# A new order for the opening of all five engines, three small inputs in one load, and the last product cut by columns

## The chip, the cores and the metric

The kernel runs on one core of one Trainium2 chip. A core has five engines that run side by side: TensorE (PE in the profile, with its weight loads as PEld), VectorE (DVE), ScalarE (ACT), GpSimd (POOL) and SyncE (SP), which here issues nearly all transfers. The metric is the time of one execution on the device, in microseconds (us); lower is better.

## The reference

Windowed attention over 8 batches, 8 heads, 576 positions and 64 dimensions, and then a dense block on its output (4608 tokens of 512, inner size 1024):

```python
scores = scale * np.matmul(q, k.transpose(0, 1, 3, 2))
mask_plain = (rel >= 0) & (rel < 32)                       # heads 0 to 3
mask_dil = (rel >= 0) & (rel < 128) & (rel % 4 == 0)       # heads 4 to 7
attn = softmax(np.where(mask, scores, -1e9)); x = attn @ v # to (4608, 512)

h = x @ w_in
sm = softmax(h); solu = h * sm
ln = (solu - mean) / sqrt(var + 1e-6) * g_ln
out = (ln @ w_out).astype(np.float32)
```

The two weights arrive as 64-bit floats. They have to be turned into 32-bit floats on the chip, by their bits.

## The kernel before

**Units.** The attention is 32 units (a batch and two heads each). The steps of unit n are written as words: `q` loads q and k, `v` loads v, `S` is the scores on PE (the mask first, as a product of the 16-bit identity `id_bf` with `mask_sb`, then 40 small products), `max`, `sub`, `exp`, `sum`, `inv`, `norm` the softmax, `turn` a transpose on VectorE (`pt`), `V` the product with v, `xh` and `xl` the split of its result into a high part on ScalarE (`x_hi`) and a low part (`x_lo`). Scores of units 0 to 4 all lie in banks 2 and 3 of the accumulator, later ones in banks 6 and 7; so `S` of a unit waits until the scores of the unit before are read. Three tuples say who does a step: units in `ACT_SCORES` have their scores copied by ScalarE (`cp`) and the maximum subtracted by GpSimd, all others have that subtraction (L291) on VectorE; units in `POOL_X` have `xl` on GpSimd after a copy by ScalarE (`xc`); blocks in `DVE_LOW` have `lo` on VectorE and all others on GpSimd.

**Weights.** They are 16 blocks, `w0` to `w7` of w_in and `w8` to `w15` of w_out, of 128 rows and 512 64-bit numbers, which is 1024 floats in a load. Each goes through `abs` and `low` (ScalarE), `clamp`, `sign` and `join` (VectorE), for w_out `gain` with the factors g (ScalarE), `hi` (ScalarE) and `lo`. The sign is taken out of the upper 16-bit quarter and written as 16-bit numbers:

```python
def conv_sign(b):
    upper = words[b].bitcast(U16).rearrange("p (n four) -> p n four", four=4)[:, :, 3]
    nc.vector.tensor_scalar(
        out=cv[b]["low"].bitcast(U16).rearrange("p (n two) -> p n two", two=2)[:, :, 1],
        in0=upper, scalar1=SIGN_BIT, scalar2=None, op0=ALU.bitwise_and,
    )
```

`SLOTS` gives each block the buffer that it is loaded to: a later block waits until its buffer's last one is converted.

**Token tiles.** The dense block is 36 tiles of 128 tokens: `ha` and `hb` are the first 512 columns of h (first and last half of the inner sum), `hc` and `hd` the others; h of tiles 0 and 2 lies in banks 0 and 1, of the other tiles up to 15 in banks 2 and 3. Then come `peak`, `e` and `gate` (which reads the banks for the last time), `mid`, `var`, `forth` and `back` (out to memory and back in another order), `trA`/`trB`, `thA`/`thB`, `tlA`/`tlB` (transpose, high and low part by halves), `o` (24 products of 512 columns with w_out) and `out`. From tile 16 on, pairs of tiles share products of half size (L733).

**Order.** Nothing is scheduled by the framework: each engine does its work in the order in which the words are written. `OPENING` is one long list of words for all five engines, up to unit 11 and tile 7; behind it the loops run `STEP` and `PAIR`, and `LAST_PAIR` for tiles 34 and 35. A list thus sets five queues at once, and a wait on an engine holds up all that stands behind it there. SyncE issues loads in the order of the list; at most eight are on their way.

## Time and profile before

| what | value |
|---|---|
| time, median of 3 runs | 502.91 us (501.33 to 503.94) |
| profiled execution: its time | 504.69 us |
| profiled execution: its span, first to last instruction | 502.8 us |
| granted clock of TensorE | 1.00 |
| busy: PE, DVE, ACT, POOL | 469.9, 351.4, 291.3, 298.7 us |
| transfers | 94.14 MB, 187 GB/s on average |

The profile is one execution. A row of a timeline has the start and the length in us, the engine, the line of the kernel, the operation, what it writes and reads, its shapes and how many; in brackets stands how long the engine was idle ahead of it, and what ended that. A row of a group has the same with the busy time and the mean of one in ns. "PE banks L255" are score products, "PE banks L333" the products with v, L247 the masks, L401 tiles of h, L531 the products with w_out. The chain of work is followed back from the last instruction, at each step to what released it; "issue" in it is time in which the engine waited for nothing that the profile shows.

### The profile page before, as it was taken

How to read it: one execution, taken by the hardware profiler on the slowest of the kernel's cores; microseconds unless marked ns; L12 is line 12 of the kernel's file. 1: busy time of each engine (PE TensorE's matmuls, PEld its weight loads, DVE VectorE, ACT ScalarE, POOL GpSimd, SP SyncE). 2: the span in 40 equal slices, each digit the busy share in tenths (PEclk: the TensorE clock that was granted, in tenths of full speed). 3: DMA queues.
4: the chain of work that ended last, by engine and by line, in shares of the span. 5: the costliest groups of instructions: out<-in, count | busy, mean ns of one | idle time of the engine just before them, and what ended most of it. 6: DMA issues, size and time to landing. Idle time of an engine off the chain costs nothing.

```text
span 502.8 us, 16542 instructions
## 1 busy us (share of the span) xinstructions
PE 469.9 (93%) x7064; PEld 376.0 (75%) x7064; DVE 351.4 (70%) x619; ACT 291.3 (58%) x483; POOL 298.7 (59%) x367
## 2 busy tenths in 40 slices
PE   1457998999999999999999999999999999999996
PEld 1336776788878888788878787878787888888875
DVE  3996989867627788777868686868676865445562
ACT  3766897744424444534457575757575767666551
POOL 1652776556533765778976666665756555766440
PEclk9999999999999999999999999999999999999999
DMA  7979175664465655666667677676765545354461
GB/s 280 402 254 359 37 261 163 230 190 133 137 193 156 194 164 169 186 175 178 201 175 216 206 211 211 210 211 211 212 210 164 160 129 146 104 168 124 113 188 63
DMA packets 51337, 94.14 MB, mean 187 GB/s; under 512 B 5952, under 2 KB 26048, under 8 KB 51264
## 3 DMA queue, kind: packets, MB, share of 16 engines
q1 hardware_dynamic: 50544, 92.43, 59.6%
q8 instruction: 55, 0.90, 0.8%
q10 hardware_dynamic: 720, 0.66, 0.4%
q14 instruction: 18, 0.15, 0.1%
HBM read 60.04 MB, written 28.31 MB: 176 GB/s over the span
## 4 chain that ended last, share of the span: by engine, by line
PE 91%; DMA 5%; issue 2%; DVE 1%; ACT 0%; SPq 0%; DVEq 0%; ACTq 0%
PE banks L531 40%; PE banks L733 20%; PE banks L401 18%; PE banks L333 7%; PE banks L255 6%; DMA qt<-qT 2%; DMA raw<-w_in 2%; DMA kt<-kT 1%; DVE pt L317 0%; PE banks L247 0%; DVE x_lo L388 0%; DVE nmax L412 0%; SPq L232 0%; DVE rs L302 0%; ACT sm L285 0%
## 5 line engine op out<-in xcount | busy, mean ns | idle before, releaser
L531 PE MATMUL banks<-w_o,th 128*128 128x512 f32 x576 | 179.9, 393 | 0.0
L522 POOL TENSOR_TENSOR tl<-t,th 128x512 fp32r<-128x512 f32 x68 | 87.9, 1305 | 59.9 <-ACT th L516 59.8
L531 PEld LDWEIGHTS banks<-w_o,th 128*128 128x128 f32 x576 | 106.6, 188 | 22.6 <-ACT th L516 0.6
L531 PE MATMUL banks<-w_o,tl 128*128 128x512 f32 x288 | 112.5, 391 | 0.0
L401 PE MATMUL banks<-w_i,x_hi 128*128 128x512 f32 x256 | 82.8, 405 | 0.2 <-DVE mu L436 0.2
L531 PEld LDWEIGHTS banks<-w_o,tl 128*128 128x128 f32 x288 | 54.0, 188 | 12.3 <-DVE tl L522 0.9
L516 ACT CAST th<-t 128x512 fp32r<-128x512 f32 x72 | 43.4, 621 | 23.5 <-DVE t L508 16.1
L401 PEld LDWEIGHTS banks<-w_i,x_hi 128*128 128x128 f32 x256 | 47.2, 191 | 11.1 <-DVE mu L436 0.8
L508 DVE STREAM_TRANSPOSE t<-raw 128x512 f32<-128x512 f32 x72 | 46.9, 684 | 6.1 <-DMA out<-ob 3.0
L401 PE MATMUL banks<-w_i,x_lo 128*128 128x512 f32 x128 | 50.7, 396 | 0.0
L333 PEld LDWEIGHTS banks<-pt,vt 32*64 32x64 f32 x2816 | 35.3, 138 | 20.0 <-issue 12.8
L452 ACT ACTIVATE e<-t 128x1024 f32<-128x1024 f32 x35 | 37.0, 1058 | 17.6 <-DVE t L448 17.3
L294 POOL TENSOR_TENSOR sm<-sm,mx 128x640 f32<-128x640 f32 x27 | 34.5, 1276 | 21.4 <-DVE mx L281 18.8
L333 PE MATMUL banks<-pt,vt 32*64 32x64 f32 (+3 forms) x2816 | 38.8, 234 | 8.6 <-issue 5.4
L298 ACT ACTIVATE sm<-sm 128x640 f32<-128x640 f32 x32 | 23.6, 739 | 35.8 <-POOL sm L294 35.1
L255 PEld LDWEIGHTS banks<-kt,qt 64*32 64x32 f32 x2560 | 29.8, 112 | 17.7 <-issue 10.7
L269 DVE TENSOR_TENSOR sm<-banks,mask_sb 128x640 f32<-128x640 f32 x22 | 18.1, 824 | 35.1 <-PE banks L255 35.0
L255 PE MATMUL banks<-kt,qt 64*32 64x64 f32 x2560 | 35.7, 238 | 5.6 <-issue 4.1
L544 ACT ACTIVATE ob<-banks,rstd 128x512 f32<-128x512 f32 x35 | 24.0, 686 | 24.8 <-issue 16.6
L757 DVE CUSTOM_DVE_ANT_0 t<-banks,t 128x512 f32<-128x512 f32 x30 | 20.7, 690 | 22.3 <-PE banks L733 16.9
L751 ACT COPY t<-banks 128x512 f32<-128x512 f32 x30 | 17.6, 588 | 30.3 <-PE banks L733 30.3
L427 ACT ACTIVATE e<-t,nmax 128x1024 f32<-128x1024 f32 x19 | 21.9, 1153 | 18.8 <-DVE nmax L764 18.2
(151 smaller groups left out, 868.5 us busy)
## 6 DMA issues: line engine op xcount, KB each, us to landing
mid<-t SPq DMA_DIRECT2D x140, 128.0 KB, 2.4
raw<-mid SPq DMA_DIRECT2D x34, 512.0 KB, 3.9
vt<-vw SPq DMA_DIRECT2D x32, 384.0 KB, 3.9
kt<-kT SPq DMA_DIRECT2D x32, 312.0 KB, 4.4
qt<-qT SPq DMA_DIRECT2D x32, 296.0 KB, 4.7
out<-ob SPq DMA_DIRECT2D x35, 256.0 KB, 2.7
x_hi<-x SPq DMA_DIRECT2D x12, 288.0 KB, 3.5
t<-w_in SPq DMA_DIRECT2D x5, 512.0 KB, 7.8
```

Source lines behind the costliest of these rows:

```text
L255: nc.tensor.matmul(out=ps[WIN * c : WIN * c + WIN, h, WQ * i : WQ * i + WQ], lhsT=qt[D * h : D * h + D, q0 : q0 + WIN], rhs=kt[D * h : D * ...
L294: eng.tensor_tensor(out=st[n]["sm"], in0=st[n]["sm"], in1=wide(mx), op=ALU.subtract)
L298: nc.scalar.activation(out=sm, in_=sm, func=AF.Exp, scale=0.125)
L333: nc.tensor.matmul(out=ps_x[D * h : D * h + D, c, c0 : c0 + k1 - k0], lhsT=vt[WIN * c : WIN * c + WIN, i, D * h : D * h + D], rhs=pt[WIN * ...
L401: nc.tensor.matmul(out=ps_h(i)[:, half], lhsT=a[:, kt, xs], rhs=w_i[:, kt, half, part, :], start=(kt == 0 and k == 0), stop=(kt == KT - 1 ...
L452: nc.scalar.activation(out=e, in_=t, func=AF.Square, accum_out=per_tile(i, "sq"))
L508: nc.vector.transpose(out=turned(i)[:, cut(c)].rearrange("p k (a r) -> p k a r", r=WIN), in_=ms[i]["mv"].rearrange("p (a k s) -> p k a s", ...
L516: nc.scalar.copy(out=ms[i]["th"][:, cut(c)], in_=turned(i)[:, cut(c)])
L522: eng.tensor_tensor(out=ms[i]["tl"][:, cut(c)], in0=turned(i)[:, cut(c)], in1=ms[i]["th"][:, cut(c)].bitcast(F32), op=ALU.subtract,)
L531: nc.tensor.matmul(out=ps_o(i), lhsT=a[:, f, :], rhs=w_o[:, f, part, :], start=(f == 0 and k == 0), stop=(f == FT - 1 and k == 2), skip_gr ...
L544: nc.scalar.activation(out=ob, in_=ps_o(i), func=AF.Copy, scale=rstd)
L733: nc.tensor.matmul(out=banks[:, bank], lhsT=left(pa, kt), rhs=right(pb, kt), start=j in (1, 2, 5) and kt == 0 and k == 0, stop=kt == 1 and ...
```

## The change

The kernel's arithmetic stays, but for the order of the last sums. Four things change: the list `OPENING` is another one, for all five engines; the tuples beside it have other members; the 16-bit identity, both masks and g come in one load `pack`, and the 32-bit identity, which nothing reads, is gone; and the last `o` (tile 35) is done by halves of columns, the left half into bank 0 and the right half into bank 1. The left half goes out while the right half is multiplied; the right half goes out in two quarters, by ScalarE and VectorE, each with its own tile and its own queue (ACT and SP).

```diff
-ACT_SCORES = (1, 5, 7, 8, 9)
-POOL_X = (0, 4, 5)
-DVE_LOW = (12, 13, 14, 15)
+ACT_SCORES = (2, 5, 6)
+POOL_X = (4, 5)
+DVE_LOW = (13,)
...
-    "w1 ib abs1 w3 m0 low1 q0 clamp1 w0 sign1 w2 abs3 q1 low3 q2 join1 hi1 S0 sign3 clamp3 "
...
+    "pack q0 S0 w0 q1 max0 sub0 low0 abs0 w3 exp0 abs3 S1 q2 clamp0 low3 sign0 sum0 w2 inv0 "
...
-    "oA.b oB.b out.b "
+    "oL.b outL.b oR.b outR.b "
...
+    packed = const.tile([P, P // 2 + NS * WQ + FT], F32, name="packed")
+    id_bf = packed[:, 0 : P // 2].bitcast(BF16)
+    mask_sb = packed[:, P // 2 : P // 2 + NS * WQ].bitcast(BF16).rearrange("p (d c) -> p d c", d=2)
+    g_sb = packed[:, P // 2 + NS * WQ :]
...
+    def moe_o_half(i, half):
+        th, tl = ms[i]["th"], ms[i]["tl"]
+        cols = slice(DO // 2 * half, DO // 2 * half + DO // 2)
+        for f in range(FT):
+            for k, (a, part) in enumerate(((th, 0), (th, 1), (tl, 0))):
+                nc.tensor.matmul(
+                    out=banks[:, half, cols],
+                    lhsT=a[:, f, :],
+                    rhs=w_o[:, f, part, cols],
...
+    def moe_out_part(i, half, cols, on_act):
+        if half == 0:
+            ob = moe.tile([P, DO], F32, name="ob", bufs=1)
+        else:
+            ob = att.tile([P, 2, NS, WQ], F32, name=f"sm{int(on_act)}")
...
+        if on_act:
+            nc.scalar.activation(out=ob[:, cols], in_=ps[:, cols], func=AF.Copy, scale=rstd)
+            nc.scalar.dma_start(out=rows[:, cols], in_=ob[:, cols])
         else:
...
+            nc.sync.dma_start(out=rows[:, cols], in_=ob[:, cols])
...
+    def out_right(i):
+        moe_out_part(i, 1, slice(DO // 2, DO * 3 // 4), True)
+        moe_out_part(i, 1, slice(DO * 3 // 4, DO), False)
```

Lines behind the edit have other numbers: the scores are L252 after (L255 before), the sign L828 (L803), the clamp L821 (L796), the join L836 (L811), `sub` on VectorE L288 (L291), `max` L278 (L281), `turn` L314 (L317), the products with w_out L528 (L531) and, by halves, L549.

SyncE at the start of the program, before. `t`, `raw` and `tp` with w_in or w_out are blocks of the weights (t1 is w1, t3 w3, t0 w0, t2 w2), sizes are partitions x 32-bit floats (16-bit for the identity and the mask):

```order
L232 DMA t1_98<-w_in 128x1024
L833 DMA id_bf_83<-ident_bf 128x128
L232 DMA t3_103<-w_in 128x1024
L835 DMA mask_sb_81<-mask 128x320
L209 DMA kt0_109<-kT 128x624
L210 DMA qt0_108<-qT 128x592
L232 DMA t0_113<-w_in 128x1024
L232 DMA t2_116<-w_in 128x1024
L209 DMA kt1_121<-kT 128x624
L210 DMA qt1_120<-qT 128x592
```

The same place after:

```order
L857 DMA packed_80<-pack 128x392
L206 DMA kt0_97<-kT 128x624
L207 DMA qt0_96<-qT 128x592
L229 DMA t0_142<-w_in 128x1024
L206 DMA kt1_145<-kT 128x624
L207 DMA qt1_144<-qT 128x592
L229 DMA t3_156<-w_in 128x1024
L206 DMA kt2_204<-kT 128x624
L207 DMA qt2_203<-qT 128x592
L229 DMA t2_213<-w_in 128x1024
L229 DMA t1_222<-w_in 128x1024
L229 DMA raw4_227<-w_in 128x1024
```

The first k and q moved from the fifth and sixth place to the second and third; w1, once the first, is the eleventh now. Behind these stand w4 (the last row), v0, w7, q3, w10, w9, w5, v1, w6, v2, v3 and q4.

VectorE around the subtraction of unit 3 and the transpose of unit 2, before (`mx`, `sm`, `rs` belong to the softmax, `mag` and `low` to the weights, `pt0_590` is unit 2's transpose):

```order
L281 TENSOR_REDUCE mx_467<-banks_90 128x10
L302 TENSOR_REDUCE rs_475<-sm0_337 128x10
L291 TENSOR_TENSOR sm1_478<-banks_90,mx_467 128x640
L306 TENSOR_SCALAR rs_475<-rs_475 128x10
L307 RECIPROCAL rs_475<-rs_475 128x10
L811 SCALAR_TENSOR_TENSOR mag2_437<-mag2_437,low2_335 128x512
L302 TENSOR_REDUCE rs_540<-sm1_478 128x10
L306 TENSOR_SCALAR rs_540<-rs_540 128x10
L307 RECIPROCAL rs_540<-rs_540 128x10
L388 TENSOR_TENSOR x_lo_89<-banks_90,x_hi_88 128x576
L317 STREAM_TRANSPOSE pt0_590<-sm0_337 128x640
```

and after (`pt0_510` is unit 2's transpose):

```order
L385 TENSOR_TENSOR x_lo_86<-banks_87,x_hi_85 128x576
L278 TENSOR_REDUCE mx_433<-banks_87 128x10
L821 TENSOR_SCALAR mag1_424<-mag1_424 128x512
L828 TENSOR_SCALAR low1_426<-raw5_370 128x512
L836 SCALAR_TENSOR_TENSOR mag0_356<-mag0_356,low0_362 128x512
L836 SCALAR_TENSOR_TENSOR mag1_424<-mag1_424,low1_426 128x512
L828 TENSOR_SCALAR low3_367<-t0_245 128x512
L821 TENSOR_SCALAR mag3_437<-mag3_437 128x512
L288 TENSOR_TENSOR sm1_502<-banks_87,mx_433 128x640
L385 TENSOR_TENSOR x_lo_86<-banks_87,x_hi_85 128x576
L314 STREAM_TRANSPOSE pt0_510<-sm0_296 128x640
```

Six instructions on weights stand now between the maximum of unit 3 and its subtraction; before, one other stood there. Ahead of that subtraction VectorE has 38 instructions besides three fills in both programs, but others: after, the scores of units 0 to 2 come ahead of most of the weights.

PE at the scores of units 8 and 9, after (kt0 and qt0 are unit 8's, kt1 and qt1 unit 9's):

```order
L398 MATMUL banks_87<-w_i_83,x_lo_86 128x512
L244 LDWEIGHTS packed_80
L244 MATMUL banks_87<-packed_80 128x320
L252 MATMUL banks_87<-kt0_1170,qt0_1169 32x64 x40
L244 LDWEIGHTS packed_80
L244 MATMUL banks_87<-packed_80 128x320
L252 MATMUL banks_87<-kt1_1283,qt1_1282 32x64 x40
L398 MATMUL banks_87<-w_i_83,x_hi_85 128x512 x2
```

S9 follows S8 at once here, with `ha5` behind it. Before, hc4, V7, ha4, hd4 and hb4 stood between the two, and o0 behind S9. Up to V2 the order of PE is the same in both programs (S0, S1, S2, V0, S3, V1, S4, V2); behind it come ha1 hc0 V3 ha0 hb0 before, and ha0 hc1 hc0 V3 ha1 hb0 after. V6 and V7 stand together now, ahead of hc4.

More of the change, by code (lines that the diff above doesn't have):

```diff
@@ L138, in windowed_attention_then_solu_kernel @@
     w_out: bass.AP,
-    g_ln: bass.AP,
-    mask: bass.AP,
-    ident: bass.AP,
-    ident_bf: bass.AP,
+    pack: bass.AP,
     out: bass.AP,
@@ L542, in moe_out @@
         rows, rstd = out[i * P : i * P + P, :], ms[i]["rstd"]
-        if i < NTILE - 1:
-            nc.scalar.activation(out=ob, in_=ps_o(i), func=AF.Copy, scale=rstd)
-            nc.sync.dma_start(out=rows, in_=ob)
-        else:
-            left, right = slice(0, DO // 2), slice(DO // 2, DO)
-            nc.scalar.activation(
-                out=ob[:, left], in_=ps_o(i)[:, left], func=AF.Copy, scale=rstd
-            )
-            nc.vector.tensor_scalar(
-                out=ob[:, right], in0=ps_o(i)[:, right], scalar1=rstd, scalar2=None, op0=ALU.mult
-            )
-            nc.scalar.dma_start(out=rows[:, left], in_=ob[:, left])
-            nc.sync.dma_start(out=rows[:, right], in_=ob[:, right])
+        nc.scalar.activation(out=ob, in_=ps_o(i), func=AF.Copy, scale=rstd)
@@ new lines, in moe_out @@
+        nc.sync.dma_start(out=rows, in_=ob)
+        del ms[i]
+    def moe_o_half(i, half):
[7 more added lines that the diff above has]
+                    rhs=w_o[:, f, part, cols],
+                    start=(f == 0 and k == 0),
+                    stop=(f == FT - 1 and k == 2),
+                    skip_group_check=True,
+                )
@@ new lines, in moe_out_part @@
+    def moe_out_part(i, half, cols, on_act):
+        if half == 0:
+            ob = moe.tile([P, DO], F32, name="ob", bufs=1)
+        else:
+            ob = att.tile([P, 2, NS, WQ], F32, name=f"sm{int(on_act)}")
+            ob = ob.rearrange("p h s w -> p (h s w)")
+        rows, rstd = out[i * P : i * P + P, :], ms[i]["rstd"]
+        ps = banks[:, half]
+        if on_act:
+            nc.scalar.activation(out=ob[:, cols], in_=ps[:, cols], func=AF.Copy, scale=rstd)
+            nc.scalar.dma_start(out=rows[:, cols], in_=ob[:, cols])
+        else:
+            nc.vector.tensor_scalar(
+                out=ob[:, cols], in0=ps[:, cols], scalar1=rstd, scalar2=None, op0=ALU.mult
+            )
+            nc.sync.dma_start(out=rows[:, cols], in_=ob[:, cols])
@@ L556, in moe_out, with out_left @@
+    def out_left(i):
+        moe_out_part(i, 0, slice(0, DO // 2), True)
+    def out_right(i):
+        moe_out_part(i, 1, slice(DO // 2, DO * 3 // 4), True)
+        moe_out_part(i, 1, slice(DO * 3 // 4, DO), False)
         del ms[i]
@@ L831, in windowed_attention_then_solu_kernel @@
         "q": load_qk, "v": load_v, "w": load_w,
-        "i": lambda _: nc.sync.dma_start(out=id_sb, in_=ident),
-        "ib": lambda _: nc.sync.dma_start(out=id_bf, in_=ident_bf),
-        "g": lambda _: nc.sync.dma_start(out=g_sb, in_=g_ln),
-        "m": lambda d: nc.sync.dma_start(out=mask_sb[:, d], in_=mask[:, d]),
+        "pack": lambda _: nc.sync.dma_start(out=packed, in_=pack),
         "abs": conv_abs, "low": conv_low, "clamp": conv_clamp, "sign": conv_sign,
@@ L952 @@
         "w_out": _bits(_by_blocks(inputs["moe_w_out"]).reshape(DF, DO)),
-        "g_ln": np.ascontiguousarray(_by_blocks(inputs["moe_g_ln"]).reshape(FT, P).T),
-        "mask": _mask().astype(ml_dtypes.bfloat16),
-        "ident": np.eye(P, dtype=np.float32),
-        "ident_bf": np.eye(P, dtype=np.float32).astype(ml_dtypes.bfloat16),
+        "pack": np.concatenate(
+            [
+                np.eye(P, dtype=ml_dtypes.bfloat16).view(np.float32),
+                _mask().astype(ml_dtypes.bfloat16).reshape(P, -1).view(np.float32),
+                np.ascontiguousarray(_by_blocks(inputs["moe_g_ln"]).reshape(FT, P).T),
+            ],
+            axis=1,
+        ),
     }
```

6 lines of the change are left out of this document (2 added, 4 removed), and 48 rows, old and new, of the table OPENING.

## The prediction

> **What bounds the kernel now.** I read first the page's head, then the chain that ended last in order of time, then table views of the opening.
>
> ```profile
> PE 469.9 (93%) x7064; PEld 376.0 (75%) x7064; DVE 351.4 (70%) x619; ACT 291.3 (58%) x483; POOL 298.7 (59%) x367
> ```
>
> TensorE (PE) is busy for 469.9 of 502.8 us, so some 33 us of the span can be had without removing a matmul. The chain tells where they lie (start, length, what):
>
> ```profile
> 2.58 7.03 DMA kt<-kT
> 9.63 7.75 DMA raw<-w_in
> 17.39 9.02 DMA qt<-qT
> ...
> 26.97 2.98 issue
> ...
> 32.47 2.56 issue
> ...
> 36.01 0.65 ACT x_hi L371
> 36.68 0.76 DVE x_lo L388
> 37.44 0.76 DVE pt L317
> ...
> 38.61 2.83 issue
> 41.44 1.47 PE banks L333 x63
> 42.91 4.48 PE banks L401 x12
> ...
> 123.80 5.44 PE banks L531 x24
> ```
>
> Up to 26.4 us the chain is loads. Then come units 3, 1, 4 and 2 of the attention with three pauses of 2.98, 2.56 and 2.83 us in which PE waits for nothing the profile names. From 42.91 us on the chain is matmuls almost without a break to 498.9. The end of the kernel is therefore the end of V2 (42.91), plus a fixed amount of matmuls, plus the breaks left after that, plus the way out. The first twelve matmuls take 4.48 us, later ones 5.44 for 24; that start-up is paid in both kernels.
>
> The loads in the opening, in stretches of 5 us (columns: PE, PEld, DVE, ACT, POOL busy, clock, DMA share, GB/s):
>
> ```profile
> 0.00:5.00 5.00, 0.00 (x0) 0.10 (x1) 0.12 (x3) 1.96 (x3) 0.19 (x4) 1.00 0.54 161
> 5.00:10.00 5.00, 0.69 (x2) 0.10 (x1) 1.66 (x4) 2.25 (x5) 0.00 (x0) 1.00 0.93 334
> 10.00:15.00 5.00, 2.39 (x114) 1.77 (x115) 4.92 (x7) 3.00 (x6) 2.62 (x2) 1.00 1.03 403
> 15.00:20.00 5.00, 2.77 (x130) 1.87 (x114) 4.91 (x9) 3.73 (x7) 3.33 (x3) 1.00 1.03 401
> ```
>
> Two things stand here: the queue is full from 10 us on, and VectorE (DVE) has 4.9 of 5 us taken from 10 us on after being nearly empty for 10. PE is waiting for VectorE's share of the opening, and VectorE starts late because two blocks of w_in are loaded ahead of the first q and k.
>
> **Part 1: the new order of loads and of VectorE.** Bytes arrive in order, so an arrival is read from their running sum: 0.81 MB by 5 us, 2.48 by 10, 4.49 by 15, 6.50 by 20. By the shapes in the order of SP a block of w is 512 KB, a pair of k and q 608, a v 384, the pack 196. The new list has the pack and q0 first: 804 KB, 0.82 MB, at 5.1 us. Before, the first score products began with q0 here:
>
> ```profile
> 8.83 0.69 PE L247 MATMUL banks<-mask_sb,id_bf 128*128 128x320 bf16 x2 [8.83 <-DMA mask_sb<-mask]
> 10.49 1.39 PE L255 MATMUL banks<-kt,qt 64*32 64x64 f32 x80 [0.97 <-DMA qt<-qT]
> 493.20 0.69 ACT L544 ACTIVATE ob<-banks,rstd 128x512 f32<-128x512 f32 x1
> L811 DVE SCALAR_TENSOR_TENSOR mag<-mag,low 128x512 int32<-128x512 int32 x8 | 7.2, 895 | 0.1
> L796 DVE TENSOR_SCALAR mag<-mag 128x512 f32<-128x512 f32 x9 | 4.1, 465 | 4.3 <-ACT mag L780 4.3
> L281 DVE TENSOR_REDUCE mx<-banks 128x10 f32<-128x640 f32 x5 | 4.0, 804 | 0.2 <-PE banks L255 0.2
> L803 DVE TENSOR_SCALAR low<-t 128x512 uint16<-128x512 uint16 x6 | 3.1, 519 | 3.2 <-ACT low L790 3.2
> L803 DVE TENSOR_SCALAR low<-raw 128x512 uint16<-128x512 uint16 x2 | 2.0, 990 | 0.0
> L803 DVE TENSOR_SCALAR low<-tp 128x512 uint16<-128x512 uint16 x1 | 1.7, 1658 | 0.0
> L306 DVE TENSOR_SCALAR rs<-rs 128x10 f32<-128x10 f32 x4 | 1.0, 260 | 0.1
> ```
>
> The first row is the two mask products of S0, the third one ScalarE pass over 512 columns. The lower seven are VectorE's groups from 5 to 43 us, with the mean of one in ns. The sign (L803 before, L828 after) has 6.8 us in 9, a mean of 0.76, though its cheapest group has 0.52 and its dearest 1.66.
>
> S0 then runs 5.1 to 6.5 us, its maximum and subtraction (0.80 and about as much) end at 8.1. w0 (1.35 MB in all) lands at 6.6; ScalarE converts it in two passes (0.69 each if they are like the row shown), so the first clamp stands at about 8.1 too. From that clamp to the maximum of unit 3 the new list has on VectorE five clamps (2.3), five signs (3.8), four joins (3.6), three maxima (2.4), seven more passes of the maximum's length (three sums, a subtraction, two transposes, an x_lo: 5.6), and three inverses of two short instructions, at 0.26 or less (1.5): 19.2 us, ending at 27.3. Then two clamps, two signs, two joins and the subtraction of unit 3 follow (5.0): 32.4. That subtraction frees the banks for S4, which takes 0.7 for the masks and 1.4 as above: 34.5, with x_lo1 and the transpose of unit 2 done beside it (1.6). Before, V2 went from 38.2, the end of its transpose, to 42.91, 4.7 us with its pause; I keep both, and V2 ends at 39.2. That is 3.7 us earlier.
>
> The other bound: the means hold the stretched signs and joins. With 0.46 for each sign and 0.69 for each join (single rows below) the two sums are 16.3 and 4.0; V1 decides then. q3 (6.23 MB) lands at 19.3; before it landed at 26.41 and V1 ended at 36.0, 9.6 later with two pauses, so V1 ends at 28.9, its x parts and the transpose at 31.2, and V2 at 35.9: 7.0 us earlier. v1 (8.2 MB) lands by the same rate at 24.2, just as S3 ends. I take 4.7, nearer the means, which come from the same work in the same stretch.
>
> A stretched and a plain sign, a plain join, and what GpSimd (POOL) did beside the stretched one:
>
> ```profile
> 5.87 0.46 DVE L803 TENSOR_SCALAR low<-t 128x512 uint16<-128x512 uint16 x1 [0.22 <-ACT low L790]
> 6.36 0.69 DVE L811 SCALAR_TENSOR_TENSOR mag<-mag,low 128x512 int32<-128x512 int32 x1
> 19.14 1.71 POOL L312 TENSOR_TENSOR sm<-sm,rs 128x640 f32<-128x640 f32 x1
> 19.66 1.52 DVE L803 TENSOR_SCALAR low<-raw 128x512 uint16<-128x512 uint16 x1
> ```
>
> So one meeting costs VectorE 1.06 us, and the sign ends as GpSimd does. [...]
>
> Work between engines: DVE_LOW gives three subtractions back to GpSimd, ACT_SCORES takes two units' subtractions to VectorE, POOL_X one x_lo to VectorE: about 2.0 off and 2.4 onto VectorE, which the lists counted above contain already. g, the masks and the identities in one load: the same 196 KB as four loads before, already in the running sum. I cost the missing issues at nothing: what hides them is the full queue; if it ran empty, each would be worth its 0.33 (the issue in part 3), 1.0 in all for three. The 64 KB identity at the end of the old list (`i`) is read by nobody.
>
> **Part 2: breaks after V2.** Before, PE's waits of any size between V2 and 100 us are these (in brackets):
>
> ```profile
> 77.62 0.43 PE L247 MATMUL banks<-mask_sb,id_bf 128*128 128x320 bf16 x2 [1.70 <-DVE x_lo L388]
> 79.22 0.73 PE L401 MATMUL banks<-w_i,x_hi 128*128 128x512 f32 x2 [0.20 <-DVE mu L436]
> 81.42 1.08 PE L333 MATMUL banks<-pt,vt 32*64 32x64 f32 x80 [0.54 <-DVE pt L317]
> 74.96 1.23 DVE L412 TENSOR_REDUCE nmax<-banks 128x1 f32<-128x1024 f32 x1 [0.88 <-PE banks L401]
> ```
>
> 2.44 us together. After, at the same place, PE does V6 (1.08) while VectorE does tile 3's peak (1.23) and unit 7's transpose (0.8): 1.0 of waiting; V7, while VectorE does x_lo6 and tile 3's gate (0.76, and a pass over 1024 columns like the peak): 0.9 more before hc4 gets its banks. New is S9 straight behind S8 in the same two banks: PE waits for unit 8's maximum and subtraction, 1.6 plus handing over, 1.7. Together 3.6, which is 1.1 more than before. From 88 us on o0 and o1 are matmul work that PE had in both lists, and I see no engine late there.
>
> **Part 3: the way out.** The last rows before:
>
> ```profile
> 51.35 0.29 PE banks L247 x2
> 498.90 0.47 ACT L548 ACTIVATE ob<-banks,rstd 128x256 f32<-128x256 f32 x1 [5.02 <-PE banks L531]
> 499.47 0.48 DVE L551 TENSOR_SCALAR ob<-banks,rstd 128x256 f32<-128x256 f32 x1 [5.43 <-ACT ob L548]
> 499.98 0.33 SPq L555 DMA_DIRECT2D out<-ob  x1
> L531 PEld LDWEIGHTS banks<-w_o,th 128*128 128x128 f32 x553 | 102.3, 188 | 21.6 <-ACT th L516 0.4
> ```
>
> VectorE's half waited for ScalarE's, and the last store was issued 1.12 us after the matmuls. Now the left half goes out beside the right half's matmuls, and the two last quarters lie in tiles of their own, so they run side by side. 512 columns cost ScalarE 0.69 and 256 cost 0.47, so 128 about 0.36: issue at 0.44, a gain of 0.7 (0.57 if a quarter costs as much as a half). Against it 48 matmuls of 256 columns replace 24 of 512 at 0.227. 320 columns take 0.145 (first row, two of them), so the line through both gives 0.118 for 256: 5.66 instead of 5.44, a loss of 0.2. The lower end is half of 0.227 (no loss); the upper is one weight load for each at its 0.188, 9.0 us, a loss of 3.6. I take 0.118, since the masks' products have their weight loads too and show no such floor. [...] No trace here shows a dense run of 256 columns.
>
> **Sum.** -4.7 + 1.1 - 0.5 = -4.1 us. The profiled execution took 504.69 with a span of 502.8; the median shown is 502.91, so that execution was 1.8 above it. 504.69 becomes 500.6, and the median 498.8 us, 0.8% less. Half a percent, 2.5 us, is about what a measurement of this kernel can tell from no change: from 500.4 to 505.4 is no change.
>
> **Rivals.** A: fewer meetings, V2 at 35.9: 2.3 better, 496.5. For it speaks that the new list starts VectorE on scores while GpSimd is still empty (0.19 and 0.00 us in the first two stretches); against it that nine signs in 38 us averaged 0.76.
> B: the narrow matmuls are held by their weight loads, 3.4 worse than summed: 502.2, no change. The 188 ns are the time of one load, not shown to be the distance of two.
> C, the other sign: VectorE's signs and joins now fall beside GpSimd more often than before, because the list is dense earlier and GpSimd has three more subtractions. Each further meeting on the way to o0 costs 1.06; four eat the gain (503), and from seven on it is slower: 506.2. VectorE was already 98% busy from 10 to 20 us; against it, its empty first 8 us are still there to be gained.
> D: the three pauses of 2.6 to 3.0 us come from something that a fuller queue makes longer; doubled, that is 8 us, and the gain is gone: 507. Against it: the three lie within 0.4 us of each other, though they fall 5 to 6 us apart in an opening whose traffic changes.
>
> **Chances.** Forecast (496.9 to 500.4) 0.50; A 0.16; B 0.12; less gain through C's first four meetings or late supply, 0.13; C past seven or D 0.09. Faster 0.66, same 0.25, slower 0.09. The range takes A and B and a little below A: 495.8 to 502.4.
>
> **What would show it.** S0 at about 5 us, the end of V2 between 36 and 39.2, the pauses at the same points of PE's program, a new wait of 1.7 us between S8 and S9, the 48 last matmuls 0.12 apart, the last store issued under 0.5 us after them. Wrong if V2 ends after 41, if PE shows breaks over 6 us from V2 to o1, or if the last product takes 9 us.

## The result, and the profile after

The changed kernel took 508.25 us (median of 6 runs, 506.87 to 509.79); the kernel before, run beside it, 502.27 (6 runs, 501.07 to 503.94). The ratio is 1.0119, with a 95% interval of 1.0088 to 1.0149: slower by about 1.2%, where 0.8% faster was forecast. The profiled execution of the changed kernel is its fastest run (506.87, span 505.1).

The chain of work that ended last, in order of time (start, length, what); the last line is the left and right half of the last product, the columns are those of the chain shown before:

```profile
37.49 5.62 PE banks L398 x18
...
57.02 5.94 DMA qt<-qT
63.10 1.04 PE banks L252 x60
...
77.48 7.48 PE banks L398 x24
...
89.97 6.38 PE banks L398 x24
96.35 10.88 PE banks L528 x48
...
496.04 5.79 PE banks L549 x46
```

V2 ends at 37.49 us, as hoped. But 24 products of h, 5.69 and 5.73 us in the first trace of before, take 7.48 and 6.38 here, and o0 starts at 96.35. TensorE's own rows behind V2 with a wait of more than a microsecond (in brackets: the wait, and what ended it):

```profile
63.10 1.03 PE L252 MATMUL banks<-kt,qt 64*32 64x64 f32 x80 [1.48 <-DMA qt<-qT]
...
74.05 0.30 PE L330 MATMUL banks<-pt,vt 32*64 32x16 f32 x8 [1.91 <-issue]
75.89 1.48 PE L330 MATMUL banks<-pt,vt 32*64 32x64 f32 x80 [1.54 <-DVE x_lo L385]
...
87.98 0.65 PE L244 MATMUL banks<-packed 128*128 128x320 bf16 x2 [1.78 <-DVE sm L288]
```

They are S7, the last products of V6, V7 and S9. With two short ones (0.23 and 0.10) TensorE waits 7.0 us from V2 to o1; before it was 2.4. The wait ahead of S7 has its cause in SyncE's queue, whose waits between 38 and 62 us were (wait, how often, the longest):

```profile
SPq L229 <- DVE low L828: 12.6, 1, 12.6
SPq L206 <- PE banks L252: 4.5, 1, 4.5
SPq L214 <- PE banks L330: 3.2, 1, 3.2
```

The load of w14 waited 12.6 us for VectorE's sign of the block that lay in its buffer, q10 for S6, v8 for V4; q7 stood behind all three, was issued at 57.02 and landed at 62.96.

The second new thing is the granted clock. Stretches of 3.41 us, cut where the clock changes (length, busy time of PE, clock, DMA share, GB/s):

```profile
60.75:64.16 3.41, 1.94 (x86) 1.00 0.95 331
70.99:74.40 3.41, 1.45 (x81) 1.00 1.02 381
74.40:77.82 3.42, 1.83 (x81) 0.50 0.97 290
77.82:81.23 3.41, 3.41 (x9) 0.50 0.89 247
81.23:84.64 3.41, 3.41 (x17) 1.00 0.46 128
84.64:88.06 3.42, 1.64 (x85) 1.00 0.44 170
88.06:91.47 3.41, 3.41 (x86) 0.50 0.76 242
```

After a stretch with 1.45 or 1.64 us of work the next one has half the clock; after a full one it is back at 1.00. The three halved stretches hold 8.65 us of work at half speed, so at most 4.3 us are lost if work takes twice as long there, an estimate. Counted by the products it is 3.5: 7.48 and 6.38 in place of 5.69 each, V7 1.48 in place of 1.08, and S9 with its masks 0.6 more.

The way out got shorter, but not in the way that was planned:

```profile
501.85 0.37 ACT L567 ACTIVATE sm<-banks,rstd 128x128 f32<-128x128 f32 x1 [2.35 <-PE banks L549]
502.32 0.35 DVE L570 TENSOR_SCALAR sm<-banks,rstd 128x128 f32<-128x128 f32 x1 [5.74 <-ACT sm L567]
502.70 0.33 SPq L573 DMA_DIRECT2D out<-sm  x1
```

From the end of the matmuls (501.8) to the end of the span it is 3.3 us; before, 498.8 to 502.8. VectorE's quarter still waited for ScalarE's: the last store was issued 0.89 us after the matmuls, where 0.44 was forecast.

### The profile page after: what moved, and what is told of

Its sections match the earlier page's. It is cut to its first block, busy times and chain, and to the rows that moved or that the text cites. A ratio compares the mean times of both kernels' runs of the same rounds, so it can differ in the third digit from the quotient of the medians.

```text
span 505.1 us, 16592 instructions
## 1 busy us (share of the span) xinstructions
PE 473.0 (94%) x7088; PEld 380.4 (75%) x7088; DVE 352.0 (70%) x619; ACT 289.0 (57%) x481; POOL 294.6 (58%) x367
## 4 chain that ended last, share of the span: by engine, by line
PE 85%; DVE 6%; DMA 5%; ACT 1%; issue 1%; SPq 1%; DVEq 0%; ACTq 0%
PE banks L528 36%; PE banks L758 20%; PE banks L398 16%; PE banks L330 6%; PE banks L252 5%; DMA raw<-w_in 1%; DMA t<-w_in 1%; DMA mid<-t 1%; DMA qt<-qT 1%; PE banks L549 1%; DVE t L433 1%; DVE low L828 1%; DVE mx L278 1%; DVE mag L836 1%; DVE mag L821 1%
## 5 line engine op out<-in xcount | busy, mean ns | idle before, releaser
L528 PE MATMUL banks<-w_o,th 128*128 128x512 f32 x560 | 175.3, 394 | 0.0
L528 PEld LDWEIGHTS banks<-w_o,th 128*128 128x128 f32 x560 | 103.7, 188 | 21.8 <-ACT th L513 0.4
L528 PE MATMUL banks<-w_o,tl 128*128 128x512 f32 x280 | 109.2, 390 | 0.0
L398 PE MATMUL banks<-w_i,x_hi 128*128 128x512 f32 x256 | 84.6, 413 | 0.1
L528 PEld LDWEIGHTS banks<-w_o,tl 128*128 128x128 f32 x280 | 52.6, 188 | 11.6 <-DVE tl L519 0.4
L398 PEld LDWEIGHTS banks<-w_i,x_hi 128*128 128x128 f32 x256 | 48.6, 196 | 11.2 <-DVE mu L433 0.2
L266 DVE TENSOR_TENSOR sm<-banks,packed 128x640 f32<-128x640 f32 x22 | 18.1, 823 | 39.2 <-PE banks L252 39.2
L291 POOL TENSOR_TENSOR sm<-sm,mx 128x640 f32<-128x640 f32 x25 | 31.5, 1261 | 22.7 <-DVE mx L278 16.9
L252 PEld LDWEIGHTS banks<-kt,qt 64*32 64x32 f32 x2560 | 30.0, 113 | 18.3 <-issue 14.2
L252 PE MATMUL banks<-kt,qt 64*32 64x64 f32 x2560 | 35.8, 241 | 6.1 <-DMA qt<-qT 4.4
L782 DVE CUSTOM_DVE_ANT_0 t<-banks,t 128x512 f32<-128x512 f32 x30 | 20.7, 690 | 22.5 <-PE banks L758 17.0
L442 ACT ACTIVATE t<-t,mu 128x1024 f32<-128x1024 f32 x23 | 26.5, 1151 | 11.0 <-DVE mu L441 11.0
```

Of the source, the lines that this page charges most:

```text
L252: nc.tensor.matmul(out=ps[WIN * c : WIN * c + WIN, h, WQ * i : WQ * i + WQ], lhsT=qt[D * h : D * h + D, q0 : q0 + WIN], rhs=kt[D * h : D * ...
L291: eng.tensor_tensor(out=st[n]["sm"], in0=st[n]["sm"], in1=wide(mx), op=ALU.subtract)
L398: nc.tensor.matmul(out=ps_h(i)[:, half], lhsT=a[:, kt, xs], rhs=w_i[:, kt, half, part, :], start=(kt == 0 and k == 0), stop=(kt == KT - 1 ...
L442: nc.scalar.activation(out=dst, in_=src, func=AF.Identity, bias=mu, scale=1.0)
L528: nc.tensor.matmul(out=ps_o(i), lhsT=a[:, f, :], rhs=w_o[:, f, part, :], start=(f == 0 and k == 0), stop=(f == FT - 1 and k == 2), skip_gr ...
```

## The experiments

Ratios are against the kernel before on the same chip, with 95% intervals. Places in the list are given by words; "behind V2" means in TensorE's order.

**q7 earlier**

```diff
-... w11 q6 hc0 lo6 v5 xl2 ... sign8 q7 join8 ...
+... w11 q6 hc0 lo6 v5 q7 xl2 ... sign8 join8 ...
```

> The changed kernel with one word moved: q7, the load of unit 7, stands straight behind v5 in the list, ahead of w14, q10, v8 and w13. Theory 'late load': SyncE held q7 back behind w14's, q10's and v8's waits; now q7 lands before 45 us, PE's 1.48 us wait ahead of S7 (63.10 in the changed kernel) is gone, S7 to V6 come 1.5 us earlier, the wait ahead of V7 shrinks; the kernel is 1.5 to 3 us faster than the changed one (506 against 508.25). Rival 'supply': VectorE and the tile's own chain (peak, e, gate) are late anyway; then the 1.48 us come back as longer waits ahead of V6, V7 or hc4, the stretch to hc4 ends within 0.5 us of 77.5, and the time stays at 508.

505.65 us, ratio 1.0043 (1.0014 to 1.0072), against 1.0119 for the change as it was. TensorE's rows with waits:

```profile
74.69 1.08 PE L330 MATMUL banks<-pt,vt 32*64 32x64 f32 x80 [1.55 <-DVE x_lo L385]
76.28 1.18 PE L398 MATMUL banks<-w_i,x_hi 128*128 128x512 f32 x2 [0.51 <-DVE mu L433]
...
86.64 0.43 PE L244 MATMUL banks<-packed 128*128 128x320 bf16 x2 [1.77 <-DVE sm L288]
98.16 0.50 PE L528 MATMUL banks<-w_o,th 128*128 128x512 f32 x1 [0.82 <-DVE w_o L850]
```

S7 waits no more and the pause in V6 shrinks to 0.41, so the late load was real: 2.6 us less than the change as it was, or 3.2 when each is set against before on its own chip (2.8 above it in place of 6.0). The wait ahead of V7 did not shrink, against my expectation, and two new ones stand at hc4 and o0: part of the gain is given back to VectorE.

**S8 apart from S9**

```diff
-... mid3 xh7 q9 hc4 var3 ... hd4 hb4 hi11 S8 ... v11 max8 sub8 ... S9
+... mid3 xh7 q9 hc4 S8 var3 ... sign12 max8 sub8 hd4 hb4 hi11 ... S9
```

> The changed kernel with S8 moved ahead, straight behind hc4, and unit 8's maximum and subtraction moved ahead of peak4 on VectorE, where it stood idle for 2.96 us; S9 no longer stands straight behind S8. Theory 'adjacency' (my step of 1.7 us): the wait of 1.78 us ahead of S9 goes, the clock does not fall at 88 us, and 1.8 + 1.3 = 3.1 us are won (505). Rival 'tile chain': ha5 needs the banks that gate4 reads, and peak4, e4 and gate4 end some 3.7 us after hb4; with only S9 (1.4) left in between, a wait of about 2.3 us appears ahead of ha5, the clock falls all the same, and the time is 507.5 to 508.5.

507.67 us, 1.0098 (1.0065 to 1.0132): the rival was right. S9 follows without a wait, and ha5 waits instead:

```profile
89.56 0.72 PE L398 MATMUL banks<-w_i,x_hi 128*128 128x512 f32 x2 [2.68 <-DVE mu L433]
```

The row names the mean behind gate4. The 1.78 us ahead of S9 covered a wait that tile 4's chain imposes anyway.

**Products that fill two waits**

```diff
+    def fill(n):
+        for _ in range(n):
+            nc.tensor.matmul(out=banks[:, 0], lhsT=x_hi[:, 0, 0:P], rhs=w_i[:, 0, 0, 0, :],
...
-... V6 var2 ... abs15 S9
+... V6 fill4 var2 ... abs15 fill5 S9
```

> The changed kernel with nine products of 512 columns added whose result nobody reads (into bank 0, between tile 2's gate and the first product with w_out): four between V6 and V7, five straight ahead of S9. They fill waits and shorten none. Theory 'clock': the granted clock is set for intervals of 3.41 us by how much TensorE worked in the one before (idle 1.91 and 1.78 of 3.41 brought 0.5, idle 1.48 and 1.70 did not); with the wait ahead of S9 filled, no fall at 88 us, and the fall at 74.4 ends one interval earlier: 2.0 to 2.3 us faster than the changed kernel (506). Rival: the clock falls for another reason (small products, or a budget over a longer time); then both falls stay and the time is 508 or a little above.

507.58 us, 1.0078 (1.0038 to 1.0117), an interval that overlaps with the change's own, so the time decides nothing. In the trace the wait ahead of S9 is 0.40 and the clock is not lowered behind it; the stretch that follows the one with this wait:

```profile
91.12:94.53 3.41, 3.41 (x73) 1.00 0.95 288
```

The fall after V6 lasted two stretches as before; that part was a miss.

**Shifting TensorE's program**, first with 32-bit products ahead of S2, then with 16-bit ones ahead of S0:

```diff
-... turn0 S2 ...
+... turn0 tiny64 S2 ...
```

```diff
-pack q0 S0 ...
+pack q0 tiny64 S0 ...
```

> The changed kernel with 64 tiny products (32 x 16, result unread) added ahead of S2, where PE waits 3.9 us for VectorE anyway. They move every later instruction of PE by 128 or more places in its program. Theory 'program fetch': the waits that the trace calls issue (1.69 ahead of S3, 1.91 in the midst of V6) come at fixed places of the program, where 16 KB of it arrive too late because small products use them up in 2 us; then the 1.91 us of V6 is gone or stands at another product, and if it is gone the clock does not fall at 74 us: 2 to 4 us faster. Rival: these waits belong to the products themselves or to a semaphore that the profile does not name; then V6 still waits 1.9 us at its last eight products and the time is 508 to 509.

511.05 us, 1.0165 (1.0129 to 1.0200). Each 32-bit product stands in the trace as two, with two weight loads (the 40 of a unit's scores are x80 in the rows above): the shift was 256 places, and V6 paused at the same eight products (1.14). Undecided, hence the second:

> The changed kernel with 64 tiny products (32 x 16, 16-bit, result unread) ahead of S0, where PE waits 2.9 us for the first q. They move every later instruction of PE by 128 places, half of the 256 places that lay between the waits without a named reason in all five traces (places 706, 961, 1217, 2753; the earlier shift was by 256 by chance, and V6 waited at the same products again). Theory 'program fetch': no such wait stands at V6's last eight products or at S3's middle; they stand 128 places earlier, or are hidden by products of 512 columns there; if V6 has none the clock does not fall at 74 us and the time is 2 to 3 us below the changed kernel, 505 to 506. Rival: the waits belong to the products: same places, 508.

515.75 us, 1.0267 (1.0234 to 1.0299): on the time I was wrong by 10 us. On the places the theory held; the clock fell at other stretches, not never. TensorE's unnamed waits above 1 us:

```profile
21.66 1.15 PE L337 MATMUL banks<-pt,vt 32*64 32x64 f32 x57 [1.82 <-issue]
...
28.59 0.45 PE L252 MATMUL banks<-kt,qt 64*32 64x64 f32 x11 [3.91 <-issue]
...
40.73 0.44 PE L337 MATMUL banks<-pt,vt 32*64 32x16 f32 x15 [3.40 <-issue]
```

V6 has none. Counting TensorE's instructions (matmuls, weight loads and waits for semaphores) ahead of each unnamed wait in the traces:

```
before              450  706  961 1217
before, 2nd trace   450  706  961 1217
changed                  706      1217                2753
q7 earlier                        1217           2497 2754
shift by 256        449  706  962      1473                3009
shift by 128        449  705  962 1218 1473                3010
```

They lie 256 apart, or a multiple of it, within a place or two, whatever stands there. The page of the changed kernel has TensorE's rows and the queue that it calls instruction (packets, MB, share):

```profile
PE 473.0 (94%) x7088; PEld 380.4 (75%) x7088; DVE 352.0 (70%) x619; ACT 289.0 (57%) x481; POOL 294.6 (58%) x367
...
q8 instruction: 55, 0.90, 0.7%
```

55 packets of 16 KB, and 14,176 matmuls and weight loads, which is 55 times 256 and a rest. I take from these counts that a packet brings a block of 256 of TensorE's instructions, and that TensorE waits at the edge of a block when small products have used up the one before it faster than the next arrives. The packets' own records agree: in the changed kernel one was under way from 71.57 to 72.57, TensorE stopped in V6 at 72.14 and went on at 74.05. In all nineteen traces each of the 84 unnamed waits above 0.15 us ends 0.9 to 1.6 us after a packet of this queue has landed (the seven in the first trace of before and in the changed kernel 1.27 to 1.50); in the first trace of before the packets of the three long ones (27.38, 32.76 and 39.14) even started after TensorE had stopped. The shift freed V6, but the edges in the opening fell on worse places: 10.0 us of unnamed waits there instead of 1.9.

**The kernel before, traced again, twice**

> The kernel before, unchanged, for a second trace: its runs lie between 500.5 and 507.4 with the mean granted clock at 0.995 to 1.0, and the one trace at hand shows 1.0 throughout. Theory: one interval of 3.41 us at clock 0.5 lies in the wait of 1.70 us near 77 us, and the end of V2 differs between executions by up to 3 us with the landing of loads; from o1 to the end both traces agree within 0.5 us. Rival: the executions differ in the second half of the kernel.

502.70 us, span 500.7. TensorE's rows at the three pauses and at S8:

```profile
29.95 1.35 PE L255 MATMUL banks<-kt,qt 64*32 64x64 f32 x75 [2.71 <-issue]
...
33.93 0.95 PE L333 MATMUL banks<-pt,vt 32*64 32x64 f32 x44 [1.19 <-issue]
...
39.24 1.47 PE L333 MATMUL banks<-pt,vt 32*64 32x64 f32 x79 [1.55 <-issue]
75.28 0.43 PE L247 MATMUL banks<-mask_sb,id_bf 128*128 128x320 bf16 x2 [1.68 <-DVE x_lo L388]
```

V2 ends at 40.70, not 42.91, by shorter pauses and not by earlier loads; from o0 to the last matmul the two traces take 410.7 and 410.3 us. As expected, the clock falls for one stretch behind the wait of 1.68 us:

```profile
73.61:77.02 3.41, 1.54 (x83) 1.00 0.85 228
77.02:80.43 3.41, 3.41 (x58) 0.50 0.03 7
```

> The kernel before, unchanged, a third trace, for where V2 ends: 42.9 us in the first trace, 40.7 in the second. Theory: the three waits for the program (8.4 us in the first trace, 5.5 in the second) differ from one execution to the next with the loads in flight, and the first trace is at the long end; then V2 ends at 40 to 42 here. Rival: 42.9 is the rule and the second trace the exception.

505.74 us, span 503.8, with the pauses long again. The chain there:

```profile
37.59 3.11 issue
...
42.16 4.14 PE banks L401 x9
```

V2 ends just past the 42 that the theory allowed. Its end at 42.2 and 42.9 thus belongs to executions of 505.7 and 504.7 us, that at 40.70 to one near the median. The length of the pauses differs between executions of one kernel by up to 1.6 us each.

**More of the list moved**

```diff
-... v5 ... V6 var2 xh6 e3 low12 xl6 gate3 V7 clamp11 ... S8 ... max8 sub8
+... v5 q7 q8 ... V6 S8 var2 xh6 e3 low12 xl6 gate3 V7 clamp11 max8 sub8 ...
```

and, in the second kernel, with exp8 behind xh7, sum8 inv8 norm8 behind xl7 and turn8 behind sign12, also

```diff
-... S9 v9 clamp15 ... o1 V8
+... S9 V8 v9 clamp15 ... o1
```

> The changed kernel with q7 and q8 loaded straight behind v5 and with S8 moved between V6 and V7 (unit 8's maximum and subtraction behind clamp11 on VectorE). V7 behind V6 waits for the reading of V6's result by ScalarE and VectorE, 1.54 us in every run so far with the two side by side. Theory 'handing over': S8 (1.5) fills that time, hc4 starts 1.5 us earlier against q7 alone, the clock does not fall at 74 to 77 us, and the wait ahead of S9 is replaced by one of 2.0 to 2.7 ahead of ha5 (as when S8 was moved alone): 1.5 to 2.5 us faster than with q7 alone, 503.5. Rival 'tile chain': hc4 waits for gate3 in any case (0.51 with q7 alone), so the 1.5 us come back there, or as a longer wait ahead of ha5: 505 to 506.

506.59 us, 1.0083 (1.0052 to 1.0114), with a wide spread (503.29 to 508.96). V7 waits 1.52 us even behind S8, and ha5 2.67: no gain over q7 alone.

> As the kernel with q7, q8 and S8 moved, and V8 with its softmax moved ahead as well, so that S9 and V8 (3.0 us of work that waits for no tile) stand between hb4 and ha5. Theory: the wait ahead of ha5 is tile 4's chain of maximum, exponent and gate, some 3.7 us from hb4; with 3.0 us of other work in it 0.5 to 1 us is left, the clock stays at 1.0, and the time is 3 us below the kernel with S8 moved (500.5), below before's 502.5. Rival: VectorE has no time for unit 8's sum and transpose ahead of peak4, gate4 ends later by 1.9, the wait only moves to V8 or ha5, and nothing is won.

509.34 us, 1.0133 (1.0108 to 1.0157): the rival was right in what came but not in its reason. Tile 4's maximum comes 2.0 us behind hb4, where it followed at once in the kernel with S8 moved; but VectorE had room, for it stood idle 1.65 us for GpSimd's `norm` of unit 8, ahead of that unit's transpose. With 3 us of other work ahead of it ha5 waits longer than ever:

```profile
87.20 0.85 DVE L314 STREAM_TRANSPOSE pt<-sm 128x640 f32<-128x640 f32 x1 [1.65 <-POOL sm L309]
...
92.76 0.72 PE L398 MATMUL banks<-w_i,x_hi 128*128 128x512 f32 x2 [3.46 <-DVE mu L433]
```

**The new list up to V2, the old one behind it**, with the tuples `ACT_SCORES = (2, 5, 7, 8, 9)` and `DVE_LOW = (12, 13, 14, 15)`; **and the other way round, only the pack and the way out**:

```diff
 ... sum3 inv3 V2
-ha0 abs6 max4 norm3 ...
+q5 w11 q6 v5 q7 w12 v4 q8 w13 low6 abs6 sign6 join7 ...
```

```diff
-w1 ib abs1 w3 m0 low1 ... m1 ... g ... i
+w1 pack abs1 w3 low1 ...
```

> The changed kernel's list up to V2, and behind it all that is still to do in the order of the list before (o0 straight behind S9, V6 and V7 apart, ScalarE copying the scores of units 5, 7, 8, 9, four of w_out's low parts on VectorE); the loads q5 w11 q6 v5 q7 w12 v4 q8 w13 stand first in that second part. Theory 'order behind V2': the loss lies in the second part alone; V2 ends 2 to 3 us earlier than in the second trace of before (40.7), the waits from V2 to o1 are 2 to 3 us as there, the clock falls once at most: 499 to 500, 3 us below before. Rival 'supply': the new first part puts scores ahead of weights, so the conversions of w_in's last and w_out's first blocks are missing later, whatever the order; then waits of 3 us or more come at V3 to hd0 or at o0, and the time is that of before or above.

503.99 us, 1.0014 (0.9993 to 1.0034): no difference to before, so the loss lies in the list behind V2 with its two tuples, as the theory had it, but the 3 us were not won. V2 ends at 38.07, and 2.07 of its lead go at once, since the first product of h here is tile 1's, in the banks of unit 4's scores:

```profile
36.60 1.47 PE L330 MATMUL banks<-pt,vt 32*64 32x64 f32 x79 [0.93 <-issue]
40.14 1.19 PE L398 MATMUL banks<-w_i,x_hi 128*128 128x512 f32 x2 [2.07 <-DVE sm L288]
```

> The changed kernel with the opening list and the three tuples of before (the pack at the place of the 16-bit identity, the other small loads left out): only the load of the small inputs and the way out differ from before. By the traces the way out costs 0.35 us more for the narrow products and saves 0.67 behind them; the pack's 196 KB ahead of q0 instead of 33 + 82 delay q0 by 0.2 and spare three issues. Theory: 0.2 to 0.6 us less than before, which is no difference that can be measured; the whole loss of the change lies in the list. Rival: the pack delays w3 and with it the first conversions, 1 us or more slower than before.

503.94 us, 1.0001 (0.9978 to 1.0024): the pack and the way out make no measurable difference.

**Tile 0 first behind V2**

```diff
-V2 ... ha1 turn3 ... hc0 ... V3 ... ha0 ... hd0 ... hc1
+V2 ha0 ... hc1 xh2 turn3 ... hc0 ... V3 ... ha1 ... hd0
```

> The spliced kernel (the new list up to V2, the old order behind it) with tile 0 first behind V2: ha0 hc1 hc0 V3 ha1 in place of ha1 hc0 V3 ha0 and hc1 behind hd0. In the spliced kernel the first product of h was tile 1's and waited 2.07 us for unit 4's scores to be read from the same banks; tile 0 lies in other banks. Theory: the 2.07 us are covered by ha0 (2.2 at the slow start), the rest stays: 2 us below the splice, 502, and 1.5 to 2 below before on the same chip. Rival 'supply': ha0 wants both parts of w0 and w2 and hc1 those of w1 and w3 earlier than the old order did, or V3 to hd0 run into a new wait, and the 2 us come back before o0: no difference to the splice.

502.13 us, 0.9999 (0.9979 to 1.0020): the rival. V2 ends at 36.93 and ha0 follows without a wait, 3.8 us before the second trace of before, but o0 starts only 0.9 earlier. The chain here:

```profile
85.62 5.69 PE banks L528 x24
```

and in the second trace of before:

```profile
86.55 5.69 PE banks L531 x24
```

VectorE's busy time from 10 to 90 us in this kernel (clock, DMA share and GB/s behind it):

```profile
10.00:90.00 80.00, 75.87 (x123) 0.98 0.77 266
```

75.9 of 80 us; in the changed kernel it is 68.9, in the second trace of before 72.9. From V2 to o0 this kernel takes 48.7 us and the second trace of before 45.9, for the same 962 matmuls. Of the 2.8 us that the lead shrinks by, 1.4 are waits (3.25 in place of 1.88; by the rows 0.7 of the 3.25 are for ScalarE, the others for VectorE). The other 1.4 fit the clock. Two products of h from this kernel, on either side of 41.93, where the record of the clock begins with 1.00:

```profile
38.31 1.05 PE L398 MATMUL banks<-w_i,x_hi 128*128 128x512 f32 x2
...
42.38 0.63 PE L398 MATMUL banks<-w_i,x_hi 128*128 128x512 f32 x2
```

They follow each other at 0.43 us ahead of that time and at 0.23 behind it. At the wider spacing they last from 36.87 to 41.93, 5.1 us, and in the second trace of before from 40.63 to 42.89, 2.3 us: a V2 that ends earlier met a clock that was not yet up.

**Products meant to keep the clock up**, 128 x 320 with the identity, result unread:

```diff
-... V1 ... S4 ...
+... fill16 V1 ... fill5 S4 ...
```

in the kernel with tile 0 first; the same with `fill6 S8`; and in the changed kernel

```diff
-... V1 ... S4 ... V7 ... S9
+... fill14 V1 ... fill7 S4 ... fill8 V7 ... fill8 S9
```

> The best order so far (new list up to V2, old behind it, tile 0 first) with 21 products added whose result nobody reads (identity by mask, 320 columns, bank 0): sixteen ahead of V1 and five ahead of S4, where PE waits 5.25 and 2.01 us. Theory 'clock': the granted clock reads 1.0 only from 41.93 us on, five microseconds after V2, and the first products of h run at half speed until then; an interval of 3.41 us full of work brings 1.0, so with the waits filled the first products run at full speed and 1.5 to 2.5 us are won: 500 against 502.1. Rival: the slow start belongs to the first products of h (their weights' parts come late, or the clock rises at a fixed time): the same time.

504.18 us, 1.0039 (1.0015 to 1.0063): a loss. Stretches around the fills:

```profile
22.14:25.55 3.41, 2.98 (x82) 1.00 0.86 200
25.55:28.97 3.42, 1.57 (x22) 1.00 0.92 357
32.38:35.79 3.41, 1.21 (x63) 1.00 1.04 400
35.79:39.21 3.42, 3.14 (x102) 0.50 1.03 397
```

The clock's record in this trace begins at 25.55 with 1.00 (earlier stretches have no record and are shown as 1.00), 16 us earlier than in the kernel without these products (41.93), behind the stretch with 2.98 us of work. So with more work ahead of it the clock rose earlier here. It falls again at 35.79 behind 1.21 us of work, just ahead of the first products of h, and is back at 42.62 only, so these run no faster than before. V2 ends at 38.12 in place of 36.93, with 3.0 us of unnamed waits ahead of it in place of 0.7: each product added, a matmul and a weight load, also moves all later instructions by two places, and the edges of the blocks fall elsewhere. How much of the loss is that, no run separates; it holds for all kernels with added products.

> As the kernel with the 21 products, with six more straight ahead of S8, where PE waits 1.55 us and the clock falls to 0.5 for one interval in a part of the runs (mean clock 0.995 to 0.997 in place of 1.0). Theory 'clock': the interval at half speed never comes, the mean clock is 1.0 in every run, 1 us more is won on the mean: 499. Rival: the fall has another reason and stays.

503.72 us, 1.0031 (1.0005 to 1.0058). In the trace (the fastest run, 501.02) the clock does not fall at S8; the mean clock of the runs was 0.986 to 0.997, not 1.0. Missed.

> The changed kernel with products of the same kind: fourteen ahead of V1, seven ahead of S4, eight ahead of V7, eight ahead of S9. No wait is shortened; only the clock is kept up. Theory: of the 6 us that the changed kernel lost, the clock has 3 to 4: 504.5 against 508.25, the mean granted clock at 0.997 or above, and the waits ahead of S7, V6, V7 and S9 filled but not gone; what is left above before is the waits themselves. Rival 'waits alone': the time stays above 507.

505.63 us, 1.0053 (1.0025 to 1.0081), clear of the 1.0119 (1.0088 to 1.0149) without fills. By the times 2.6 us of the loss went. The fall at 88 us is absent in the trace, but its mean clock is 0.990, not 0.997, and o0 starts no earlier than about 95.6, so by what way the time fell is not shown.

**The two waits that were left**

```diff
-... V6 var2 exp7 xh6 peak3 forth2 e3 sum7 xl6 lo11 gain12 S8 inv7 gate3
+... V6 S8 peak3 var2 e3 gate3 exp7 xh6 forth2 sum7 xl6 lo11 gain12 inv7
```

and in the second also

```diff
-... V4 hb1 v7 ... xl4 S6
+... V4 hb1 S6 v7 ... xl4
```

> The best order so far (new list up to V2, old behind it, tile 0 first) with S8 straight behind V6 in the list and tile 3's maximum, exponent and gate (with tile 2's square ahead) ahead of V6's reading on VectorE and ScalarE. In every trace of the old order S8 waits 1.54 to 1.70 us for the reading of V6's result, though unit 7's scores are long read, and hc4 0.2 to 0.5 for gate3 behind it. Theory 'place in the list': S8 follows V6 at once, hc4 waits 1.2 us for gate3 in all in place of 2.0, no clock fall near 76 us: 1 to 2 us less than 502.1, just under before. Rival: S8 waits for unit 7's scores after all, or gate3's chain is longer than 3.8 us from hd3: the same 502.

503.91 us, 1.0034 (1.0011 to 1.0057). S8 follows V6 at once and hc4 waits 1.14, as expected; then V7 waits for its transpose, which VectorE does late, and nothing is won:

```profile
78.72 1.33 PE L330 MATMUL banks<-pt,vt 32*64 32x64 f32 x80 [2.35 <-DVE pt L314]
```

> The same with S6 straight behind hb1 in the list, ahead of V4's reading: S6 waited 0.68 us for that reading by ScalarE. Theory: 0.7 us less again, 500 to 501. Rival: V4's reading then waits for S6, V5 or the gate of tile 0 come later, and nothing is won: as the kernel with S8 moved.

504.45 us, 1.0041 (1.0023 to 1.0058): the rival again. No order that was tried beats the kernel before.

## Why the prediction was wrong, step by step

**Part 1, the end of V2: near in its time, partly by luck, and counted twice in the total.** I forecast 38.2 (4.7 before 42.91); it was 37.49. The way there was another one. The scores of S0 began at 6.84, not 5.1, so a landing read off the sum of bytes came out too early. v1 held V1 up until 28.98, where I had it landing at 24.2: its load was issued at 22.29 only, behind loads of weights that waited 7.6 us in all for VectorE's signs. S4 began at 33.45, 1.0 later than summed. What made up for this are the three pauses: 8.4 us before, which I had kept whole, and 1.9 here. (The second sum of the other bound is 16.9, not 16.3; V1 decides in either case.) The trace I started from was a late execution, and the sum ended with "504.69 becomes 500.6, and the median 498.8": that takes the 1.8 us which this execution lay above the median off the end. They lay in the stretch that the change removes: V2's end is 2.2 us and the time 2.0 us lower in the second trace. Against that trace (V2 at 40.70, 502.70 us) the gain is 3.2.

**Part 2, the breaks behind V2: the step that failed.** Forecast 3.6 us, measured 7.0, past the 6 that I had named as the limit. The sum had three terms, and two waits were not in it.

- S9 behind S8, 1.7: measured 1.78.
- V7, 1.0 for unit 7's transpose: measured 1.54, for another reason. The transpose was done at 73.49, but V7 writes the banks that ScalarE and VectorE read V6's result from, and waits for both; I had let it run beside x_lo6.
- hc4, 0.9 for tile 3's gate: measured 0.10, since V7 came so late that the gate ran beside it.
- S7, 1.48, was put at nothing: I listed SyncE's order at its start and did not follow it behind v5, where one word's wait holds all the words behind it. (It is the error of v1 in part 1 once more.)
- V6, 1.91, was put at nothing too: an edge of the program's blocks falls into it (in the third trace of before, 0.42).

The three terms and a short wait of 0.23 make 3.65, as summed, though two of them only by errors that cancel. The two waits that were not in the sum make 3.39, and that is the excess. Where the row named a wait, as for S9, it was right and yet not worth its length: taken away, it came back as 2.68 ahead of ha5.

**The clock: no term.** The sum has nothing for the clock, which read 1.00 in the first trace. That is no property of the kernel but of its waits. Behind waits of 1.91 and 1.78 us in the changed kernel (V6 and S9) and of 1.68 in the second trace of before, each within one stretch of 3.41 us, the next stretch had half the clock. In the first trace of before the wait of 1.70 us was split:

```profile
73.49:76.91 3.42, 2.44 (x87) 1.00 0.80 197
76.91:80.32 3.41, 2.50 (x87) 1.00 0.58 162
```

There the clock stayed at 1.00. In the second trace the wait was not split, and the clock fell once. The changed kernel waits three times like that (1.91 ahead of the end of V6, 1.54 ahead of V7, where the clock stayed at 0.50, and 1.78 ahead of S9), and lost 3.5 us; the second trace of before lost 1.4 by the same count.

**Part 3, the way out: right in one number, wrong in the way and in the net.** The stores gained 0.7 as forecast, but not since the quarters run side by side: VectorE's waits for ScalarE's in every trace with this way out, as the halves did before. Both read one bank; tiles of their own did not part them, and whether the bank is the reason no run shows. The issue of the last store came 0.3 earlier in place of 0.7, and the last store itself took 0.4 less from its issue to the end (2.36 in place of 2.78), which I had not counted: that the two make 0.7 is luck. Against it, 46 narrow products in 5.79 us are 0.126 each, forecast 0.118, which is 0.35 more than before in place of 0.2, and a wait of 0.23 for the low part came on top. The net is 0.1 in place of 0.5, in accord with the kernel in which only the pack and the way out were changed. Rival B is excluded: no sign of 0.188 each.

**The budget.** Against the second trace of before (span 500.7, after 505.1): V2 -3.2, waits 7.0 less 1.9 is +5.1, the clock 3.5 less 1.4 is +2.1, narrow products +0.35 and their wait +0.2, stores -0.7: together +3.9 of 4.4. By their times the two traced runs are 4.2 apart, the medians 6.0: the run of the change lies 1.4 below its median, that of before 0.4 above. The 1.8 in the runs without a trace, and by what way the fills took 2.6 off, stay open.

**Rivals.** A, V2 at 35.9, came half true: 37.49. C, more VectorE stalls beside GpSimd, has the right sign (in the first 45 us of the changed kernel the three signs that met GpSimd's work took 1.51 to 1.55 us and ended 0.32 behind it, the six others 0.45 to 0.48), but the traces exclude it: up to 97 us VectorE's 16 signs and 16 joins took 22.5 us in the changed kernel and 24.7 to 26.5 in the three traces of before. D named the pauses; in the opening they got shorter, and the one in V6 got long. That o0 and o1 "are matmul work that PE had in both lists, and I see no engine late there" held in the changed kernel, but only behind its other waits: in the kernel with q7 earlier o0 waits 0.82 for VectorE's part of w_out.

## What to carry to other kernels

A list for several queues is only as good as its slowest head: after any move, follow each transfer queue past the first wait, and ask what stands behind it. A short wait can have two prices, its length and what it does to the clock of the stretch behind it (here 1.78 us ahead of S9, and then 3.41 us at 0.50); a wait for a chain that another wait covers has neither, until the cover is taken away. And before a gain is taken off a median, look in a second trace whether the profiled execution was late in just the stretch that the change shortens.
